# A mixture-of-experts kernel: low halves behind the weights' chunks, gates' transfers on another queue, transposes one turn sooner

## The chip, the cores and the metric

One core of one Trainium2 chip. The metric is the device time of one execution in microseconds (us). Of the engines TensorE (PE) multiplies, VectorE (DVE) and ScalarE (ACT) work element by element, GpSimd (POOL) does some small work and issues gathers, and SyncE (SP) issues most transfers. Each engine takes its instructions in the order in which the program lists them, and so does each engine's queue of transfers.

## The reference

Three stages follow each other. Only the second one is touched by the change.

```python
x = linear_attention(q, k, v, lam)            # (1536, 512), chunks of 128 tokens here
xn = x / (norm(x) + 1e-6); en = emb / (norm(emb) + 1e-6)
logits = xn @ en.T / tau                      # 8 experts
e = argmax(logits); gate = softmax(logits)[e]
for e in range(8):                            # experts: 512 -> 1024 -> 512
    out[mask] = gate * (relu(x[mask] @ w1[e]) @ w2[e])
h = out @ w_in                                # last MLP: 512 -> 2048 -> 512
y = elu(h) @ w_out
```

## The kernel before

Matrices that have to be exact to nearly float32 are held as two float16 parts, a high and a low half; one product is three matmuls (high by high, high by low, low by high). So each result that feeds another product is evicted twice: ACT writes the high half, and DVE, which reads that high half, writes the low half (`scalar_tensor_tensor`, L951 after the first layer, L988 after the second). The weights come as float32 in 1 MB pieces (`raw`) and are split in the same manner, in chunks of 128x1024: ACT writes the high half (L151), DVE the low half (L155). An expert has four pieces, two of `w1` (4e, 4e+1) and two of `w2` (4e+2, 4e+3); the last MLP's weights come as 64-bit numbers, and DVE first joins their bits in three instructions (L214, L217, L220).

`preparing` is a generator that lays these chunks one by one into the program; one step issues the high half of a chunk and the low half of the chunk before it. When a piece is finished its `end` issues the load of a later piece on SP's queue, which waits there until the buffer of the raw piece is free (five buffers, `rawp`). `tick(t)` gives a budget of `t` us and takes steps until it is spent: 1.6 after each of the four groups (`fp`) of the first layer, 3.7 after each of the two groups (`mp2`) of the second layer. `need(i)` takes further steps if a piece has not been laid out when matmuls use it.

The loop runs layer1(0), layer1(1), layer2(0), layer1(2), layer2(1), and so on, to layer1(7), layer2(6), layer2(7). In the profile L942 is the matmuls of the first layer (96 of an expert, 24 in a group) and L981 those of the second (96, 48 in a group). The tokens of an expert are gathered from DRAM by POOL (`gather`, L762, two tiles `g`) and are then transposed to `x`: for the experts 0 and 1 on PE, for the later ones by two transposing DMAs of SP (L921). `transpose(e+1)` and `gather(e+2)` are issued in layer1(e), after the second group (for e=0 after the third). A gather waits until the transposes of two experts before have read its buffer.

`route_sorted` (a second generator, `self.sorting`) works out each token's place and gate. One piece of it is taken after every other group of layer1 (the second and the fourth). One of them, taken after layer1(1), copies the counts and adds them up (L780 to L787), the one after layer1(5) writes the gates to DRAM (`cd`, L877) and reads them back to all partitions (`bc`, L880); both transfers are on SP's queue. The last MLP multiplies by `bc` first in L1033.

The sums of the experts go into `yT` (two tiles of 128 x 3520 four-byte words), which POOL sets to zero (L962) after the third group of layer1(0). `yT` is the first tile that is laid into the memory that the attention leaves; the attention's first pool there was `io`, four buffers of 8192 bytes per partition for the tiles `in`, against 28160 bytes of the two `yT`.

Of the kernel before, what the change touches and what calls it, by code (L numbers as in the profile page):

```python
# [9 lines left out]
F32 = mybir.dt.float32  # L10
# [10 lines left out]
P = 128  # L21
B, H, S, D = 2, 8, 768, 64
NP = H // 2
N, DM, E, FE, FF = 1536, 512, 8, 1024, 2048
# [40 lines left out]
class K:  # L65
# [702 lines left out]
    def route_sorted(self, a1, rhs, ps_r):  # L768
        nc, rt, cp = self.nc, self.rt, self.cp
# [39 lines left out]
        y = a1.tile([P, NS], F32, name="y")  # L809
# [64 lines left out]
        cs = a1.tile([44, P], F32, name="cs")  # L874
        nc.vector.tensor_copy(cs[32:44], sq[32:44])  # L875
        cd = self.dp.tile([12, P], F32, name="cd")
        nc.sync.dma_start(cd, cs[32:44])  # L877
        self.bc = cp.tile([P, N], F32, name="bc")
        ct = cd[:, :]
        nc.sync.dma_start(self.bc, bass.AP(tensor=ct.tensor, offset=ct.offset, ap=[[0, P], [1, N]]))  # L880
        yield
        self.overflow_table(a1)
        if "idx" in self.dbg:
# [6 lines left out]
    def moe_mlp(self, ctx):  # L890
        tc, nc = self.tc, self.nc
# [10 lines left out]
        def mm(shape, name):  # L902

            i = next(mms) % 4
            return self.ps_x.tile(shape, F32, name=name, tag=("xp", "kr")[i]) if i < 2 else ps_m.tile(shape, F32, name=name, tag="mm")

        W = N + CAP
        yT = []
        for hl in range(2):
            y = yp.tile([P, KD, W], F16, name=f"yT{hl}")  # L910
            yT.append(y)
        rhs = rp.tile([P, NS, 60], BF16, name="rhs")
        X, HT = self.X, {}

        def transpose(e):
            x = self.xp.tile([P, 2 * KD, CAP], F16, name=f"x{e}", tag="x")
            for j, n in ((0, P), (1, REM)):
                g = self.G.pop((e, j))
                o = x[:, :, j * P : j * P + n]
                if e > 1:  # L920
                    nc.sync.dma_start(o, g[:n].rearrange("p a d -> p (a d)"), transpose=True)  # L921
                    continue

                pt = ps_a.tile([P, 2 * KD, P], F16, name=f"pt{j}_{e}", tag="acc")
                for k in range(2 * KD):
                    nc.tensor.transpose(pt[:, k, :n], g[:n, k, :], self.id16[:n, :n])  # L926
                nc.scalar.activation(out=o, in_=pt[:, :, :n], func=AF.Copy)
            X[e] = x

        def layer1(e):  # L930
            x = X.pop(e)
            h = hp.tile([P, 2, E, CAP], F16, name=f"h{e}", tag="h")
            for fp in range(4):
                ps = mm([P, 2, CAP], f"ph{e}_{fp}")
                for j in range(2):
                    f = 2 * fp + j
                    w = self.need(4 * e + f // 4)
                    c = (f % 4) * P
                    n = 0
                    for k in range(KD):  # L940
                        for wl, xl in ((0, 0), (0, 1), (1, 0)):
                            nc.tensor.matmul(  # L942
                                ps[:, j, :], w[:, wl, k, c : c + P], x[:, xl * KD + k, :], start=(n == 0), stop=(n == 11)
                            )
                            n += 1
                    if e == 0 and f == 1:
                        self.route_end(ps_a)
                        self.tick(3.0)
                f2 = slice(2 * fp, 2 * fp + 2)
                nc.scalar.activation(out=h[:, 0, f2], in_=ps, func=AF.Relu)  # L950
                nc.vector.scalar_tensor_tensor(  # L951
                    out=h[:, 1, f2], in0=ps, scalar=0.0, in1=h[:, 0, f2], op0=ALU.max, op1=ALU.subtract
                )
                if fp % 2:
                    self.finished(4 * e + fp // 2)
                if e + 1 < E and fp == (1 if e else 2):
                    transpose(e + 1)
                    if e + 2 < E:
                        self.gather(e + 2)
                if e == 0 and fp == 2:  # L960
                    for y in yT:
                        nc.gpsimd.memset(y.bitcast(F32), 0.0)  # L962
                if e > 0 and fp % 2:
                    next(self.sorting, None)
                self.tick(1.6)
            HT[e] = h

        def layer2(e):
            h = HT.pop(e)
            offs = []  # L970
            for eng in (nc.scalar, nc.vector):
                offs.append(0 if e == 0 else eng.value_load(self.offi[0:1, e : e + 1], min_val=0, max_val=N))
            for mp2 in range(2):
                ps = ps_a.tile([P, 2, CAP], F32, name=f"py{e}_{mp2}", tag="acc")
                for j in range(2):
                    c = (2 * mp2 + j) * P
                    n = 0
                    for f in range(8):
                        w = self.need(4 * e + 2 + f // 4)
                        for wl, hl in ((0, 0), (0, 1), (1, 0)):  # L980
                            nc.tensor.matmul(  # L981
                                ps[:, j, :], w[:, wl, f % 4, c : c + P], h[:, hl, f, :], start=(n == 0), stop=(n == 23)
                            )
                            n += 1
                m2 = slice(2 * mp2, 2 * mp2 + 2)
                ya, yv = (yT[0][:, m2, bass.ds(o, CAP)] for o in offs)
                nc.scalar.activation(out=ya, in_=ps, func=AF.Copy, scale=EV_Y)  # L987
                nc.vector.scalar_tensor_tensor(  # L988
                    out=yT[1][:, m2, bass.ds(offs[1], CAP)], in0=ps, scalar=EV_Y, in1=yv, op0=ALU.mult, op1=ALU.subtract
                )  # L990
                if mp2 == 1:
                    self.finished(4 * e + 2, 4 * e + 3)
                self.tick(3.7)

        self.sorting = self.route_sorted(rp, rhs, ps_a)
        for e in range(E + 1):
            if e < E:
                layer1(e)
            if e > 0:
                layer2(e - 1)  # L1000
# [318 lines left out]
```

## Time and profile before

| | |
|---|---|
| median of 3 runs | 508.62 us (508.29 to 512.58) |
| profiled execution | 509.62 us, of which the span of the trace 507.8 us |
| PE busy in the span | 471.9 us (93%) |
| DVE, ACT, POOL busy | 347.1, 224.4, 77.1 us |
| mean granted TensorE clock | 0.979 |

The span is the time from the first to the last instruction of the trace. Times in rows are counted from the span's start. The attention lies before about 92 us, the experts from 92 to 250, the last MLP after that.

### The profile page before, as it was taken

How to read it: one execution, taken by the hardware profiler on the slowest of the kernel's cores; microseconds unless marked ns; L12 is line 12 of the kernel's file. 1: busy time of each engine (PE TensorE's matmuls, PEld its weight loads, DVE VectorE, ACT ScalarE, POOL GpSimd, SP SyncE). 2: the span in 40 equal slices, each digit the busy share in tenths (PEclk: the TensorE clock that was granted, in tenths of full speed). 3: DMA queues.
4: the chain of work that ended last, by engine and by line, in shares of the span. 5: the costliest groups of instructions: out<-in, count | busy, mean ns of one | idle time of the engine just before them, and what ended most of it. 6: DMA issues, size and time to landing. Idle time of an engine off the chain costs nothing.

```text
span 507.8 us, 9088 instructions
## 1 busy us (share of the span) xinstructions
PE 471.9 (93%) x3671; PEld 330.6 (65%) x3671; DVE 347.1 (68%) x625; ACT 224.4 (44%) x374; POOL 77.1 (15%) x67
## 2 busy tenths in 40 slices
PE   7788885998999999979999999999999999999992
PEld 6677775997999999979844444444444444445561
DVE  2467795466999988996878797978845335435352
ACT  1255344174686676423265354534333342433441
POOL 4456431351011310000000000000000002001111
PEclk9899898998999999999999999999999999999998
DMA  7999933267999999893622222000000001101101
GB/s 223 363 411 420 416 109 137 86 155 251 336 346 231 368 378 302 335 342 121 214 85 83 84 83 84 1 1 1 0 1 0 1 0 43 41 1 42 43 28 61
DMA packets 28335, 79.07 MB, mean 156 GB/s; under 512 B 13280, under 2 KB 15360, under 8 KB 22144
## 3 DMA queue, kind: packets, MB, share of 16 engines
q1 hardware_dynamic: 25848, 71.42, 41.4%
q0 software_dynamic: 2112, 6.82, 4.1%
q8 instruction: 31, 0.51, 0.4%
q10 hardware_dynamic: 328, 0.19, 0.1%
q14 instruction: 16, 0.13, 0.1%
HBM read 68.57 MB, written 7.10 MB: 149 GB/s over the span
## 4 chain that ended last, share of the span: by engine, by line
PE 77%; DVE 5%; DMA 3%; SPq 1%; issue 1%; ACT 1%; POOL 0%; POOLq 0%; DVEq 0%
PE pf L1023 25%; PE po L1063 24%; PE ph L942 14%; PE py L981 13%; DMA x<-g 2%; DVE w L155 1%; SPq L921 1%; DVE stm L352 1%; DMA g<-rows,idx 1%; PE px L712 1%; DMA out<-o,idx 1%; DVE S L422 0%; DVE row L452 0%; PE st L344 0%; PE pt L926 0%
## 5 line engine op out<-in xcount | busy, mean ns | idle before, releaser
L1023 PE MATMUL pf<-yT,w 128*128 128x512 f16 (+2 forms) x672 | 133.2, 349 | 0.0
L1063 PE MATMUL po<-w,g 128*128 128x512 f16 x576 | 133.1, 379 | 0.0
L1023 PEld LDWEIGHTS <-w 128*128 128x128 f16 x672 | 62.4, 98 | 65.4
L1063 PEld LDWEIGHTS <-g 128*128 128x128 f16 x576 | 55.9, 98 | 65.5 <-DVE g L1049 0.5
L1033 DVE TENSOR_TENSOR et<-pf,bc 128x512 f32<-128x512 f32 (+2 forms) x56 | 34.4, 614 | 91.5 <-PE pf L1023 91.4
L1034 ACT ACTIVATE eu<-et 128x512 f32<-128x512 f32 (+2 forms) x56 | 31.9, 569 | 140.0 <-DVE et L1033 140.0
L942 PE MATMUL ph<-x,w 128*128 128x224 f16 x768 | 75.2, 259 | 4.0 <-DMA x<-g 2.9
L981 PE MATMUL py<-h,w 128*128 128x224 f16 x768 | 76.6, 262 | 2.2 <-DVE w L155 2.2
L155 DVE SCALAR_TENSOR_TENSOR w<-raw,w 128x1024 f16<-128x1024 f32 x64 | 76.7, 1228 | 0.1
L981 PEld LDWEIGHTS <-w 128*128 128x128 f16 x768 | 74.2, 99 | 3.4 <-DVE w L155 2.4
L942 PEld LDWEIGHTS <-w 128*128 128x128 f16 x768 | 73.4, 98 | 4.7 <-DMA x<-g 3.1
L151 ACT ACTIVATE w<-raw 128x1024 f16<-128x1024 f32 x64 | 64.9, 1049 | 4.2 <-DVE cs L875 2.4
L1082 POOL DMA_INDIRECT out<-o,idx x12 | 11.8, 986 | 307.1 <-DVE o L1080 283.6
L762 POOL DMA_INDIRECT g<-rows,idx x16 | 22.1, 1383 | 84.3 <-DMA x<-g 58.8
L1049 DVE SCALAR_TENSOR_TENSOR g<-et,g 128x512 f16<-128x512 f32 (+2 forms) x56 | 34.1, 608 | 0.2 <-ACT g L1043 0.2
L1042 DVE SCALAR_TENSOR_TENSOR et<-eu,et 128x512 f32<-128x512 f32 (+2 forms) x56 | 33.9, 606 | 0.3 <-ACT eu L1035 0.3
L1035 ACT ACTIVATE eu<-eu 128x512 f32<-128x512 f32 (+2 forms) x56 | 31.9, 570 | 1.8
L1043 ACT ACTIVATE g<-et 128x512 f16<-128x512 f32 (+2 forms) x56 | 30.9, 553 | 0.3 <-DVE et L1042 0.3
L950 ACT ACTIVATE h<-ph 128x448 f16<-128x448 f32 x32 | 17.3, 541 | 21.4 <-PE ph L942 17.2
L951 DVE SCALAR_TENSOR_TENSOR h<-ph,h 128x448 f16<-128x448 f32 x32 | 19.8, 617 | 10.0 <-ACT h L950 9.9
L151 ACT ACTIVATE w<-cv 128x1024 f16<-128x1024 f32 x16 | 16.8, 1050 | 14.3 <-DVE cv L220 14.3
L987 ACT ACTIVATE yT<-py 128x448 f32 (+1 forms) x16 | 8.7, 545 | 32.2 <-PE py L981 32.2
(183 smaller groups left out, 403.4 us busy)
## 6 DMA issues: line engine op xcount, KB each, us to landing
raw<-w SPq DMA_DIRECT2D x32, 1024.0 KB, 7.9
in<-qkv SPq DMA_DIRECT2D x20, 512.0 KB, 7.6
raw<-wi SPq DMA_DIRECT2D x8, 1024.0 KB, 6.5
raw<-wo SPq DMA_DIRECT2D x8, 1024.0 KB, 7.9
rows<-row SPq DMA_DIRECT2D x15, 256.0 KB, 6.4
win<-qkv SPq DMA_DIRECT2D x4, 512.0 KB, 9.5
bc<-cd SPq DMA_DIRECT2D x1, 768.0 KB, 4.3
Dm<-Z SPq DMA_DIRECT2D x1, 512.0 KB, 3.9
```

The costliest lines, as they stand in the source:

```text
L151: nc.scalar.activation(out=o[0], in_=x, func=AF.Copy, scale=sc)
L155: nc.vector.scalar_tensor_tensor(out=o[1], in0=x, scalar=sc, in1=o[0], op0=ALU.mult, op1=ALU.subtract)
L942: nc.tensor.matmul(ps[:, j, :], w[:, wl, k, c : c + P], x[:, xl * KD + k, :], start=(n == 0), stop=(n == 11))
L981: nc.tensor.matmul(ps[:, j, :], w[:, wl, f % 4, c : c + P], h[:, hl, f, :], start=(n == 0), stop=(n == 23))
L1023: nc.tensor.matmul(ps[:, :n], w[:, wl, k, c : c + P], yT[yl][:, k, t0 : t0 + n], start=(i == 0), stop=(i == 11))
L1033: nc.vector.tensor_tensor(out=t[:, :n], in0=UT[m, f][:, :n], in1=self.bc[:, t0 : t0 + n], op=ALU.mult)
L1034: nc.scalar.activation(out=u[:, :n], in_=t[:, :n], func=AF.Relu, scale=-1.0)
L1035: nc.scalar.activation(out=u[:, :n], in_=u[:, :n], func=AF.Exp, scale=-1.0)
L1042: nc.vector.scalar_tensor_tensor(out=t, in0=u, scalar=-1.0, in1=t, op0=ALU.add, op1=ALU.max)
L1043: nc.scalar.activation(out=g[:, 0, :n], in_=t, func=AF.Copy, scale=S_G)
L1049: nc.vector.scalar_tensor_tensor(out=g[:, 1, :n], in0=t, scalar=S_G, in1=g[:, 0, :n], op0=ALU.mult, op1=ALU.subtract)
L1063: nc.tensor.matmul(acc[t], g[:, gl, t * P : t * P + P], w[:, wl, f % 4, :], start=(f == first and i == 0), stop=(f == last and i == 2),)
```

## The change

The low half after each group of either layer (L951, L988) is issued behind the `tick` of its group, and so behind the chunks that the tick lays out; in layer1 the pieces of `sorting` and the transposes and the next gather also come ahead of it. `transpose(e+1)` and `gather(e+2)` are issued after the first group instead of the second (for e=0 as before after the third). The two transfers of the gates go to GpSimd's queue. The zeros of `yT` are written as soon as `yT` exists, ahead of layer1(0).

```diff
@@ route_sorted
-        nc.sync.dma_start(cd, cs[32:44])
+        nc.gpsimd.dma_start(cd, cs[32:44])
         self.bc = cp.tile([P, N], F32, name="bc")
         ct = cd[:, :]
-        nc.sync.dma_start(self.bc, bass.AP(tensor=ct.tensor, offset=ct.offset, ap=[[0, P], [1, N]]))
+        nc.gpsimd.dma_start(self.bc, bass.AP(tensor=ct.tensor, offset=ct.offset, ap=[[0, P], [1, N]]))
@@ moe_mlp
             y = yp.tile([P, KD, W], F16, name=f"yT{hl}")
+            nc.gpsimd.memset(y.bitcast(F32), 0.0)
             yT.append(y)
@@ layer1
                 nc.scalar.activation(out=h[:, 0, f2], in_=ps, func=AF.Relu)
+                if fp % 2:
+                    self.finished(4 * e + fp // 2)
+                if e + 1 < E and fp == (0 if e else 2):
+                    transpose(e + 1)
+                    if e + 2 < E:
+                        self.gather(e + 2)
+                if e > 0 and fp % 2:
+                    next(self.sorting, None)
+
+                self.tick(1.6)
                 nc.vector.scalar_tensor_tensor(
                     out=h[:, 1, f2], in0=ps, scalar=0.0, in1=h[:, 0, f2], op0=ALU.max, op1=ALU.subtract
                 )
-                if fp % 2:
-                    self.finished(4 * e + fp // 2)
-                if e + 1 < E and fp == (1 if e else 2):
-                    transpose(e + 1)
-                    if e + 2 < E:
-                        self.gather(e + 2)
-                if e == 0 and fp == 2:
-                    for y in yT:
-                        nc.gpsimd.memset(y.bitcast(F32), 0.0)
-                if e > 0 and fp % 2:
-                    next(self.sorting, None)
-                self.tick(1.6)
@@ layer2
                 nc.scalar.activation(out=ya, in_=ps, func=AF.Copy, scale=EV_Y)
+                if mp2 == 1:
+                    self.finished(4 * e + 2, 4 * e + 3)
+                self.tick(3.7)
                 nc.vector.scalar_tensor_tensor(
                     out=yT[1][:, m2, bass.ds(offs[1], CAP)], in0=ps, scalar=EV_Y, in1=yv, op0=ALU.mult, op1=ALU.subtract
                 )
-                if mp2 == 1:
-                    self.finished(4 * e + 2, 4 * e + 3)
-                self.tick(3.7)
```

## Rows read from the trace of the kernel before

**Rows 1.** PE's waits: engine, line, whom it waited for: us in total, times, longest.

```profile
PE ph L942 <- DMA x<-g: 2.9, 1, 2.9
PE py L981 <- DVE w L155: 2.2, 1, 2.2
```

**Rows 2.** Timeline 106 to 123 us (start, us, engine, instruction, count; idle before and releaser).

```profile
111.23 1.05 ACT L151 ACTIVATE w<-raw 128x1024 f16<-128x1024 f32 x1
...
112.89 0.17 PE L777 MATMUL op<-ms,c 128*128 128x8 f16 x1
...
113.09 0.54 ACT L950 ACTIVATE h<-ph 128x448 f16<-128x448 f32 x1 [0.81 <-PE op L777]
113.67 0.62 DVE L951 SCALAR_TENSOR_TENSOR h<-ph,h 128x448 f16<-128x448 f32 x1 [0.55 <-ACT h L950]
114.21 0.15 DVE L780 COPY cnt<-op 128x8 f32<-128x8 f32 x1
...
115.92 2.35 DVE L155 SCALAR_TENSOR_TENSOR w<-raw,w 128x1024 f16<-128x1024 f32 x2
117.19 9.12 PE L981 MATMUL py<-h,w 128*128 128x224 f16 x76 [2.19 <-DVE w L155]
```

**Rows 3.** Stretches: us, busy of PE, PEld, DVE, ACT, POOL, PEclk, DMA share, GB/s.

```profile
115.00:117.10 2.10, 0.00 (x0) 0.00 (x0) 1.96 (x8) 0.53 (x1) 0.92 (x1) 1.00 0.73 128
...
117.80:121.20 3.40, 3.40 (x23) 2.75 (x21) 0.47 (x1) 0.00 (x0) 0.92 (x1) 0.55 0.98 393
...
222.00:225.00 3.00, 2.94 (x31) 2.97 (x32) 3.00 (x4) 1.09 (x2) 0.00 (x0) 1.00 0.95 393
```

**Rows 4.** Timeline 170 to 223 us: SP's queue, POOL, and the matmuls that wait.

```profile
170.05 5.87 SPq L921 DMA_TRANSPOSE x<-g  x2
...
180.07 1.60 POOL L762 DMA_INDIRECT g<-rows,idx  x1 [9.68 <-DMA x<-g]
...
194.99 0.64 SPq L877 DMA_DIRECT2D cd<-cs  x1
...
201.99 3.49 DVE L155 SCALAR_TENSOR_TENSOR w<-raw,w 128x1024 f16<-128x1024 f32 x3
203.94 0.35 SPq L880 DMA_DIRECT2D bc<-cd  x1
...
204.39 1.44 SPq L133 DMA_DIRECT2D raw<-wi  x2
...
205.92 1.61 SPq L133 DMA_DIRECT2D raw<-wo  x2
205.93 1.21 DVE L155 SCALAR_TENSOR_TENSOR w<-raw,w 128x1024 f16<-128x1024 f32 x1
...
207.63 9.00 SPq L921 DMA_TRANSPOSE x<-g  x2
...
222.06 9.36 PE L942 MATMUL ph<-x,w 128*128 128x224 f16 x96 [2.90 <-DMA x<-g]
```

**Rows 5.** Two stretches in the same columns as rows 3: SP waits for the gates, then not.

```profile
203.00:205.00 2.00, 2.00 (x23) 2.00 (x22) 2.00 (x3) 2.00 (x4) 0.00 (x0) 1.00 0.15 33
...
207.00:209.00 2.00, 2.00 (x23) 2.00 (x22) 1.79 (x9) 0.55 (x2) 0.00 (x0) 1.00 1.01 352
```

**Rows 6.** POOL's timeline, 82 to 183 us.

```profile
82.95 0.92 POOL L762 DMA_INDIRECT g<-rows,idx  x1 [0.30 <-issue]
95.73 0.97 POOL L762 DMA_INDIRECT g<-rows,idx  x1 [11.86 <-DVE idx L755]
...
100.40 6.03 POOL L962 MEMSET yT<- 128x3520 f32 x2
...
166.81 3.58 POOL L762 DMA_INDIRECT g<-rows,idx  x1 [0.30 <-issue]
```

**Rows 7.** Timeline 249 to 253 us: the end of the experts.

```profile
250.50 0.63 DVE L988 SCALAR_TENSOR_TENSOR yT<-py,yT 128x448 f32 x1 [0.86 <-ACT yT L987]
...
252.90 0.68 DVE L1033 TENSOR_TENSOR et<-pf,bc 128x512 f32<-128x512 f32 x1
```

## What the change is predicted to do

> **What bounds the kernel now.** Read PE first: it is busy for 93% of the span, so a change in the experts can only give back time in which PE stands still or runs at a low clock. The list of PE's own waits [rows 1] has two of size there: 2.9 us on a transposed `x`, and 2.2 us on the low half of a weights' chunk. The timeline places both. The weights' wait lies early in layer2(0), 115.00 to 117.19 [rows 2]; the other before layer1(7), 219.16 to 222.06 [rows 4]. After 250 us PE goes from matmul to matmul, and nothing in this change moves work there that PE waits for. A table of stretches, read last, shows what the clock made of the gaps: behind the first it was granted at 0.55 for 3.40 us (mostly its lower level, 1.2 GHz instead of 2.4), behind the longer second one it stayed at 1.00 [rows 3].
>
> **The low halves behind the chunks.** Nothing is added or removed; DVE's order changes. What is late at 117.19 is the first of the two L155 at 115.92 [rows 2]; it takes 2.35 / 2 = 1.18 us, ends at 117.10, and PE starts 0.09 later. Its input was there long before: ACT's half ended at 111.23 + 1.05 = 112.28. In front of it on DVE stand the low half of the last group (L951 at 113.67, which had waited for ACT) and the sums of the counts, 114.21 to 115.92 = 1.71 us. The sums need only the matmul L777, which ended at 112.89 + 0.17 = 113.06; ACT was released by it at 113.09, and I take 113.10 for DVE. With the low half behind, the chain is 113.10 + 1.71 + 1.18 + 0.09 = 116.08. The wait shrinks from 2.19 to 1.08: **gain 1.1 us**. Between 0 (DVE comes late from the groups before) and 2.19 I stay with 1.1, because the rows give every link. Late next are the sums of the counts, which stay in front.
>
> The clock comes on top. The 76 matmuls behind the gap take 9.12 us [rows 2]; 96 at the full clock take 9.36 us [rows 4], so 76 take 7.41. The low clock cost 1.7 us. With half the gap I expect it not to fall: **gain 1.7 us**, bounds 0 and 1.7, in the profiled execution. A 2.90 us gap left the clock alone, so the same gap may do so in another execution.
>
> The same order in every other group costs nothing. A low half of layer 1 now comes up to one or two chunks (1.2 us each) later; layer2(e) reads it after layer2(e-1) and layer1(e+1), two times 9.4 us further on, and the four buffers for these sums are taken again only in the next layer1. In layer 2 the second and third chunk of a tick also wait for ACT's halves, which queue behind ACT's eviction, so the low half can come some 4 us after its matmuls (0.54 + 2 x 1.05 + 1.2 + 0.1); only the last MLP reads it. The last one, after layer2(7), is where this cover ends. Today it runs from 250.50 to 251.13, with DVE idle for 0.86 us before it [rows 7], about when the eighth matmul of the MLP wants it. Now a chunk of 1.2 us and the first instruction of the next one stand ahead of it. Their inputs are there a group earlier, so I expect them in DVE's idle time and a cost of nothing; uncovered it is up to 1.9 us.
>
> **The gates' transfers.** On SP's queue `bc` waits until `cd` has landed: from the issue of `cd` at 194.99 to 203.94 nothing else is issued [rows 4]. The loads behind it go out in one burst, four of 1 MB from 204.39 to 207.53, and the transposes of expert 7 behind these at 207.63. The DMA engines show it: 33 GB/s in 203 to 205, then 352 in 207 to 209 [rows 5], so 4 MB are some 12 us of work in front of those transposes. They land at 222, 14.4 us after their issue began. For comparison, those of 170.05 were all read by POOL's gather at 180.07, 10.0 us [rows 4]. On POOL the two transfers stand behind the last gather and before nothing until the outputs. Their price there isn't in the trace; the nearest rows are POOL's gathers, 0.92 to 3.58 us each [rows 6], so 1.8 to 7.2 us of an idle engine. Even with some 12 us for the landing of each the gates are there before 225, and L1033 reads them at 252.90 [rows 7]: free.
>
> **The transposes a turn sooner.** For expert 7 they pass the tick of the first group, and with it one load, the fourth of the burst; its L155 ended at 205.93 + 1.21 = 207.14, and the transposes waited for that as well. They stay behind the third load, whose buffer the L155 run of 201.99 to 205.48 frees. So they go out at about 205.0 to 205.9 instead of 207.63, with less in front of them. 205.9 + 10.0 to 14.4 is 215.9 to 220.3, against 219.16 when PE wants them. I take the short end, as the queue will not have stood idle: **gain 2.9 us**; at the long end 1.8. Everything up to there hangs on PE's groups through ACT, so a PE that comes earlier brings the transposes earlier too; where they hold still, 216 stands against 216.4. For experts 2 to 6 nothing waits now, and a turn (2.3 us) more is cover. The load that falls behind the transposes goes out up to 9 us later. That is hidden by five raw buffers, and by weights that are ready well ahead after the first experts. The gathers go along a turn sooner and pass nothing on POOL.
>
> One rule speaks against the reason just given. The Trainium skill, "DMA: Bandwidth & Descriptors", section "Issuing engines are not separate DMA queues", says that transfers from any engine share the same DMA engines and that another issuer saves only sequencer time, usually small. Here the sequencer's time is 9 us of waiting on a landing, which the rule does not count; if only the issues of 0.64 and 0.35 us counted, the transposes' gain would be nearer rival B than my sum.
>
> **The zeros first.** The two memsets (6.03 us) move from 100.40 to behind the gather of 82.95, so to about 83.9 to 89.9, if the memory is free; it is that of the attention's `in` tiles, which none of its last steps reads. POOL then stands idle until 95.73 [rows 6]: free. The gather for expert 3 no longer waits for them, but PE doesn't want it.
>
> **Sum.** 1.1 + 1.7 + 2.9 = 5.7 us: 509.62 becomes 503.9 in the profiled execution (span 507.8 to 502.1). The median of the runs lies 1.0 below that execution. If that is the clock's doing there, only 1.1 + 2.9 = 4.0 is left, 504.6; if not, 5.7, 502.9. I forecast the middle, **503.7**.
>
> **Rivals.**
> A, forecast, 502.9 to 504.6: chance 0.58.
> B, the transposes are no earlier in effect: the DMA engines are busy anyway (share 1.01, [rows 5]), and the 2.9 us stay. 508.62 - 1.1 = 507.5 to 508.62 - 2.8 = 505.8, middle 506.6. Against it speaks the 33 GB/s stretch. Chance 0.14. The Trainium skill's sentence on issuing engines, above, would put the result here.
> C, the weights' wait stays whole, since the sums are the real chain or the chunk's DVE slot slips: 508.62 - 2.9 = 505.7. Against it: each link has its row. 0.08.
> D, more: the typical run also loses the clock at the longer gap, or the first wait goes whole: 508.62 - 5.7 - 1.1 = 501.8, and with 1.7 for the clock instead of the 1.1, 501.2. 0.14.
> E, slower: the memsets hold POOL. If their memory comes free only with the attention's end, they stand in front of the gather of expert 1 (95.73), whose transposes on PE come next in line. It decides when they start later than 95.73 - 6.03 = 89.7; the price is up to 6.0 us, and about 1.7 for the clock. With the transposes' 2.9 back and the weights' wait covered: 508.62 + 7.7 - 4.0 = 512.3. For it: both are in one queue, in this order. Against it: the `in` tiles were there, and they are done early. 0.06.
>
> **How the numbers follow.** A measurement of this kernel tells about 1% from no change: 503.5 and 513.7 are the bounds. Of A some 0.4 lies below 503.5 (0.23), D wholly (0.14): faster 0.37. E reaches 513.7 only with another mishap: of its 0.06 I give 0.04 to slower. The rest, 0.59, is within 1%. The range of 501.6 to 506.9 holds A, C, two thirds of B and half of D, 0.82.
>
> **What will show it.** Right: the L155 before the second group of matmuls of layer2(0) starts near 114.8, and PE's wait on `w` L155 is about 1.1; PEclk is 1.0 from 117 to 122; PE has no wait on `x<-g`; the transposes of expert 7 go out before the fourth load; the memsets stand at 84 to 90; the first L1033 comes at about 247 instead of 252.90. Wrong: a wait of PE on L988 at the MLP's start, on the gather of expert 1, or on `x` of another expert; or a low clock in a new place.

## The result and the profile after

| | before | after |
|---|---|---|
| median of 20 runs each | 509.17 us (505.70 to 514.35) | 504.47 us (500.06 to 509.91) |
| ratio, 95% interval | | 0.9899 (0.9876 to 0.9923) |
| profiled execution, its span | 509.62 us, 507.8 us | 506.57 us, 504.8 us |
| mean granted clock | 0.979 | 0.973 |
| experts: first matmul of layer1(0) to first of the last MLP | 157.3 us (92.37 to 249.66) | 150.9 us (91.93 to 242.86) |

The ratio makes it 5.1 us faster, between 3.9 and 6.3; the medians lie 4.7 apart. The ratios here leave out executions over 1.5% above the fastest of their kernel (4 of the 20 after); the medians count all. The forecast of 503.7 was a gain of 4.9.

PE's waits in the kernel after (engine, tile, line, whom it waited for: us in total, times, longest), those that lie in the experts:

```profile
PE py L980 <- DVE w L155: 1.1, 1, 1.1
...
PE ph L943 <- DVE x L742: 0.3, 1, 0.3
```

Against [rows 1]: the wait on the transposes is gone, and that on the chunk's low half is 1.1 us instead of 2.2. What lies between is in the timeline of the kernel after (start, us, engine, instruction, count; idle before and releaser):

```profile
82.82 6.03 POOL L911 MEMSET yT<- 128x3520 f32 x2
95.42 0.98 POOL L762 DMA_INDIRECT g<-rows,idx  x1 [6.57 <-DVE idx L755]
...
111.94 0.17 PE L777 MATMUL op<-ms,c 128*128 128x8 f16 x1
...
112.17 0.17 DVE L780 COPY cnt<-op 128x8 f32<-128x8 f32 x1 [1.13 <-PE op L777]
...
113.89 2.35 DVE L155 SCALAR_TENSOR_TENSOR w<-raw,w 128x1024 f16<-128x1024 f32 x2
115.17 7.46 PE L980 MATMUL py<-h,w 128*128 128x224 f16 x76 [1.13 <-DVE w L155]
116.17 0.62 DVE L962 SCALAR_TENSOR_TENSOR h<-ph,h 128x448 f16<-128x448 f32 x1
...
190.35 0.57 POOL L877 DMA_DIRECT2D cd<-cs  x1 [13.16 <-DVE cs L875]
192.82 3.94 SPq L133 DMA_DIRECT2D raw<-wi  x2
196.21 0.59 POOL L880 DMA_DIRECT2D bc<-cd  x1 [5.28 <-DMA cd<-cs]
199.89 0.33 SPq L133 DMA_DIRECT2D raw<-wo  x1
200.32 5.08 SPq L922 DMA_TRANSPOSE x<-g  x2
205.50 0.96 SPq L133 DMA_DIRECT2D raw<-wo  x1
...
215.26 9.36 PE L943 MATMUL ph<-x,w 128*128 128x224 f16 x96
...
243.64 0.63 DVE L990 SCALAR_TENSOR_TENSOR yT<-py,yT 128x448 f32 x1 [1.34 <-ACT yT L986]
245.65 0.69 DVE L1032 TENSOR_TENSOR et<-pf,bc 128x512 f32<-128x512 f32 x1 [1.38 <-PE pf L1022]
```

It is read from the top. The memsets (now L911) stand at 82.82 to 88.85, and the gather of expert 1 behind them waits for its indices, not for them. The sums of the counts (from L780) are now released by the matmul L777; L155 follows at once, and the low half of the last group (now L962) comes behind it at 116.17. Here the copy waits for PE, where in [rows 2] it stood behind a low half. The same 76 matmuls take 7.46 us instead of 9.12. On POOL, `bc` stands for 5.28 us until `cd` has landed; SP's loads meanwhile go out from 192.82 on. The transposes of expert 7 start at 200.32, 14.9 us before layer1(7) wants them, and ahead of the fourth load; before it was 11.5 us (207.63 to 219.16, [rows 4]). The second of them landed 6.1 us after its issue, some 6 us before 215.26. The first L1032 comes at 245.65, 7.25 sooner than in [rows 7].

The table of stretches (us, busy of PE, PEld, DVE, ACT, POOL, PEclk, DMA share, GB/s) answers to [rows 3] and [rows 5]:

```profile
82.00:86.00 4.00, 2.62 (x16) 2.03 (x16) 2.45 (x10) 1.58 (x4) 4.00 (x3) 0.50 0.35 115
...
115.20:122.50 7.30, 7.30 (x77) 7.30 (x78) 5.57 (x7) 3.38 (x4) 0.00 (x0) 1.00 0.80 288
203.00:205.00 2.00, 2.00 (x23) 2.00 (x21) 1.69 (x11) 0.80 (x2) 0.00 (x0) 1.00 1.07 431
```

The first row is taken up at the end. Behind the gap PEclk is 1.00, and in the stretch that moved 33 GB/s it is 431.

**Where the gain goes.** In the profiles the experts are 6.4 us shorter and the MLP starts 6.8 us sooner, but the span is only 3.0 shorter. The MLP is no longer than it was: PE's last group of matmuls starts at 489.15 instead of 495.96, again 6.8 sooner. The rest is lost behind PE, at the scatters of the output. The timeline of the kernel after, that last group and the last three scatters:

```profile
489.15 2.90 PE L1062 MATMUL po<-w,g 128*128 128x512 f16 x12
...
486.57 0.97 POOL L1081 DMA_INDIRECT out<-o,idx  x1 [2.52 <-DVE g L1048]
491.57 0.97 POOL L1081 DMA_INDIRECT out<-o,idx  x1 [4.03 <-DVE g L1048]
495.57 0.97 POOL L1081 DMA_INDIRECT out<-o,idx  x1 [3.03 <-DMA out<-o,idx]
```

The same in the timeline of the kernel before:

```profile
495.96 2.90 PE L1063 MATMUL po<-w,g 128*128 128x512 f16 x12
...
493.39 0.97 POOL L1082 DMA_INDIRECT out<-o,idx  x1 [2.52 <-DVE g L1049]
497.20 0.97 POOL L1082 DMA_INDIRECT out<-o,idx  x1 [2.85 <-DVE g L1049]
500.85 0.97 POOL L1082 DMA_INDIRECT out<-o,idx  x1 [2.68 <-DMA out<-o,idx]
```

After stood 4.03 us where before stood 2.85, and from its last scatter to the end of the span are 9.2 us, not 7.0. The row names DVE, but the start fits the landing of the scatter before it: the one of 486.57 landed at 490.80, 0.77 us before the next starts, and in the kernel before the landing was at 496.43, again 0.77 before 497.20. From PE's last matmul to the end of the span that makes 12.7 us after and 9.0 before. I call it the tail; whether it belongs to the kernel is among the questions below.

### The profile page after: what moved, and what is told of

It reads as the page before. It is cut to its first block, busy times and chain, and to the rows that moved or that the text cites. A ratio compares the mean times of both kernels' runs of the same rounds, so it can differ in the third digit from the quotient of the medians.

```text
span 504.8 us, 9102 instructions
## 1 busy us (share of the span) xinstructions
PE 472.4 (94%) x3671; PEld 331.9 (66%) x3671; DVE 347.1 (69%) x625; ACT 224.7 (45%) x374; POOL 75.8 (15%) x69
## 4 chain that ended last, share of the span: by engine, by line
PE 78%; DVE 5%; DMA 3%; issue 1%; POOL 0%; ACT 0%; POOLq 0%; DVEq 0%; ACTq 0%
PE pf L1022 25%; PE po L1062 24%; PE py L980 14%; PE ph L943 13%; DMA g<-rows,idx 1%; DVE w L155 1%; DMA rows<-row 1%; DMA out<-o,idx 1%; DVE row L452 1%; DVE S L422 0%; DVE stm L352 0%; PE st L344 0%; PE tm L429 0%; PE px L712 0%; DVE ohb L660 0%
## 5 line engine op out<-in xcount | busy, mean ns | idle before, releaser
L1032 DVE TENSOR_TENSOR et<-pf,bc 128x512 f32<-128x512 f32 (+2 forms) x56 | 34.4, 614 | 93.3 <-PE pf L1022 93.2
L155 DVE SCALAR_TENSOR_TENSOR w<-raw,w 128x1024 f16<-128x1024 f32 x64 | 77.4, 1229 | 7.5 <-ACT w L151 7.4
L980 PE MATMUL py<-h,w 128*128 128x224 f16 x768 | 74.9, 259 | 1.1 <-DVE w L155 1.1
L1081 POOL DMA_INDIRECT out<-o,idx x12 | 12.1, 1011 | 287.6 <-DVE o L1079 262.9
L762 POOL DMA_INDIRECT g<-rows,idx x16 | 19.4, 1211 | 81.4 <-DMA x<-g 61.8
L951 ACT ACTIVATE h<-ph 128x448 f16<-128x448 f32 x32 | 17.2, 541 | 18.0 <-PE ph L943 17.2
L962 DVE SCALAR_TENSOR_TENSOR h<-ph,h 128x448 f16<-128x448 f32 x32 | 19.8, 618 | 5.8 <-ACT h L951 5.3
```

The costliest lines, as they stand in the source:

```text
L155: nc.vector.scalar_tensor_tensor(out=o[1], in0=x, scalar=sc, in1=o[0], op0=ALU.mult, op1=ALU.subtract)
L980: nc.tensor.matmul(ps[:, j, :], w[:, wl, f % 4, c : c + P], h[:, hl, f, :], start=(n == 0), stop=(n == 23))
L1032: nc.vector.tensor_tensor(out=t[:, :n], in0=UT[m, f][:, :n], in1=self.bc[:, t0 : t0 + n], op=ALU.mult)
```

## The experiments

The theory: the change gives back three things, half of the chunk's wait (1.1), the low clock behind it (1.7) and the wait on the transposes (2.9). Its rivals: one part does it all, or the clock or the wait of the transposes is a matter of the execution. Four kernels do one part alone, four take one part back, two move something further, and both kernels were profiled once more. Each ratio is to runs of the kernel before on the same chip (medians 508.70 to 511.09).

| kernel | median, us | ratio (95%) | experts, us | wait on `w`, us | wait on expert 7's `x`, us | low clock behind | tail, us |
|---|---|---|---|---|---|---|---|
| before | 509.17 | | 157.3 | 2.2 | 2.9 | `w` | 9.0 |
| before, again | 514.59 (one run) | | 159.5 | 2.2 | 3.3 | both | 12.1 |
| low halves only | 505.93 | 0.990 (0.987 to 0.993) | 155.6 | 1.1 | 3.1 | `x` | 9.4 |
| gates only | 506.14 | 0.993 (0.990 to 0.995) | 153.5 | 2.2 | 0 | `w` | 9.6 |
| turn only | 505.34 | 0.992 (0.989 to 0.996) | 151.7 | 2.2 | 0 | none | 9.5 |
| zeros only | 508.56 | 0.997 (0.993 to 1.000) | 157.0 | 2.2 | 3.4 | `x` | 9.3 |
| all but gates | 504.42 | 0.991 (0.987 to 0.994) | 150.7 | 1.1 | 0 | none | 9.3 |
| all but turn | 503.76 | 0.989 (0.985 to 0.993) | 150.6 | 1.1 | 0 | none | 9.0 |
| all but low halves | 506.20 | 0.995 (0.991 to 0.998) | 153.3 | 2.2 | 0 | `w` | 11.8 |
| all but layer 2's low halves | 505.75 | 0.989 (0.986 to 0.993) | 151.5 | 1.2 | 0 | none | 9.6 |
| after | 504.47 | 0.990 (0.988 to 0.992) | 150.9 | 1.1 | 0 | none | 12.7 |
| after, again | 507.88 (one run) | | 151.5 | 1.1 | 0 | none | 12.3 |
| sorting behind the tick | 504.36 | 0.991 (0.988 to 0.995) | 149.4 | 0 | 0 | none | 9.7 |
| gates on ACT | 505.83 | 0.992 (0.988 to 0.995) | 151.5 | 1.1 | 0 | none | 8.9 |

The columns from the fourth on are from one profiled execution of each kernel, which need not be a typical one: with the low halves alone it was the slowest of nine (509.02 us), with the sorting behind the tick the fastest of seven (501.91). A low clock means that the matmuls behind that gap took 1.5 to 1.7 us longer than at the full clock.

**One part alone.** The low halves, in layer1 (the same move in layer2):

```diff
-                nc.vector.scalar_tensor_tensor(
-                    out=h[:, 1, f2], in0=ps, scalar=0.0, in1=h[:, 0, f2], op0=ALU.max, op1=ALU.subtract
-                )
...
                 self.tick(1.6)
+                nc.vector.scalar_tensor_tensor(
+                    out=h[:, 1, f2], in0=ps, scalar=0.0, in1=h[:, 0, f2], op0=ALU.max, op1=ALU.subtract
+                )
```

> Only the low halves stand behind the ticks; transposes, gates and zeros as before. My theory (the weights' wait at layer2(0) is DVE's order): PE's wait on w L155 falls from 2.2 to about 1.1 us and the clock stays at its upper level behind it (1.7 us in an execution in which it fell before). The gates' transfer is issued some 2 us sooner, since its copy no longer stands behind a low half, so the wait on the transposed x of expert 7 shrinks too, to between 0.5 and 2 us. In all 2 to 4.5 us faster. Rival (the gain is the SP queue's alone): the wait on w stays at 2 us or more and the time falls by less than 1 us.

Timeline of this kernel, the two waits and SP's queue before the second:

```profile
116.10 7.46 PE L981 MATMUL py<-h,w 128*128 128x224 f16 x76 [1.12 <-DVE w L155]
...
190.87 0.72 SPq L877 DMA_DIRECT2D cd<-cs  x1
199.98 0.35 SPq L880 DMA_DIRECT2D bc<-cd  x1
...
204.06 9.74 SPq L921 DMA_TRANSPOSE x<-g  x2
...
219.49 10.82 PE L942 MATMUL ph<-x,w 128*128 128x224 f16 x96 [3.14 <-DMA x<-g]
```

The chunk's wait is halved and the clock holds behind it, as the theory has it. I had expected the second wait to shrink to 0.5 to 2 us, and that failed: 3.14. From the issue of `cd` to that of `bc` SP took 9.1 us again (190.87 to 199.98), so the transposes went out 3.6 us sooner than in [rows 4] and were wanted 2.8 sooner; the second landed 15.3 us after the first one's issue. And this time the clock fell there: 10.82 us for 96 matmuls that take 9.36 at the full clock.

The gates' two transfers:

```diff
-        nc.sync.dma_start(cd, cs[32:44])
+        nc.gpsimd.dma_start(cd, cs[32:44])
...
-        nc.sync.dma_start(self.bc, bass.AP(tensor=ct.tensor, offset=ct.offset, ap=[[0, P], [1, N]]))
+        nc.gpsimd.dma_start(self.bc, bass.AP(tensor=ct.tensor, offset=ct.offset, ap=[[0, P], [1, N]]))
```

> Only the gates' two transfers go to GpSimd's queue. My theory (SP stood behind the gates' landing): the loads of the last MLP go out as their buffers come free, the transposes of expert 7 are issued at the same time as before or up to 0.5 us sooner (they still stand behind the fourth load) but land within 11 us instead of 14.4, and PE's wait on them falls from 2.9 to below 0.6 us; the wait on w stays at 2.2. 2.3 to 2.9 us faster. Rival, the rule that issuing engines share the same transfer engines: the transposes land no earlier than 1 us before, the wait stays at 1.9 us or more.

Timeline of this kernel:

```profile
116.12 9.12 PE L981 MATMUL py<-h,w 128*128 128x224 f16 x76 [2.20 <-DVE w L155]
...
206.51 5.72 SPq L921 DMA_TRANSPOSE x<-g  x2
...
217.87 7.35 PE L942 MATMUL ph<-x,w 128*128 128x224 f16 x75
```

The transposes go out only 1.1 us sooner than in [rows 4], at 206.51, but the loads ahead of them had gone out from 197.53 on instead of in one burst. Each lands 6.2 to 9.0 us after its own issue, the second at 216.22, and layer1(7) starts without a wait. It is close: some 1.6 us.

The turn:

```diff
-                if e + 1 < E and fp == (1 if e else 2):
+                if e + 1 < E and fp == (0 if e else 2):
```

> Only the transposes and gathers come a turn sooner. My theory: SP still stands until about 204 behind the gates, then three loads and the transposes of expert 7 at about 206.4 instead of 207.6 with 3 MB instead of 4 in front of them; PE's wait on them falls from 2.9 to between 0.5 and 1.7 us, the wait on w stays at 2.2. 1.2 to 2.4 us faster. Rival (the turn is what counts): the wait on the transposes is gone, 2.9 us faster.

Timeline of this kernel:

```profile
116.43 7.46 PE L981 MATMUL py<-h,w 128*128 128x224 f16 x76 [2.20 <-DVE w L155]
...
200.50 0.35 SPq L880 DMA_DIRECT2D bc<-cd  x1
...
202.53 9.71 SPq L921 DMA_TRANSPOSE x<-g  x2
212.34 0.52 SPq L133 DMA_DIRECT2D raw<-wo  x1
...
216.51 8.69 PE L942 MATMUL ph<-x,w 128*128 128x224 f16 x89
```

A miss on the other side: I had left a wait of 0.5 to 1.7 us, and there was none, as the rival had it. SP still stands until 200.50, and the first transpose still takes 12.4 us from issue to landing; but they pass one load and go out 14.0 us before layer1(7), not 11.5, and that is enough. So each of the two parts takes the whole wait alone, and their gains don't add. The line at 116.43 shows something else: 2.20 us of waiting, and the clock holds.

The zeros:

```diff
             y = yp.tile([P, KD, W], F16, name=f"yT{hl}")
+            nc.gpsimd.memset(y.bitcast(F32), 0.0)
...
-                if e == 0 and fp == 2:
-                    for y in yT:
-                        nc.gpsimd.memset(y.bitcast(F32), 0.0)
```

> Only the zeros of yT are written ahead of layer1(0). My theory: the two memsets stand at about 84 to 90, the gather of expert 1 starts at 95.7 as before, nothing else moves; no change within 0.3%. Rival (POOL's memset holds DVE's small operations or the gather of expert 1): PE reaches layer1(0) or the transposes of expert 1 up to 3 or 6 us later and the time rises by as much.

The memsets ran from 84.80 to 90.83, the gather of expert 1 came at 96.52 with its wait on the indices, and both of PE's waits stood as before. The ratio of 0.9965 just leaves out 1 (0.9997), and the profile shows nothing to which 1.8 us could be put down.

**One part taken back.** The whole change with the two `nc.gpsimd` back on `nc.sync`; with `fp == (1 if e else 2)`; with both low halves back in front of their `tick`:

> The whole change, but the gates' transfers stay on SP's queue. If the turn alone carries the transposes of expert 7 (as in the run with the turn only, where PE did not wait and they landed close to the need), PE's wait on them stays at or below 0.5 us, but they land 13 to 15 us after their issue instead of some 9 as in the whole change; the time is that of the whole change within 0.3%. If the gates are needed once PE comes 1.1 us sooner, the wait comes back with 1 to 3 us. The wait on w is 1.1 us.

> The whole change, but transposes and gathers after the second group as before. If the gates' move alone carries the transposes (as in the run with the gates only, landed 1.6 us before the need), PE's wait on x stays at or below 0.5 us and the time is that of the whole change within 0.3%. If the margin of 1.6 us doesn't hold with PE 1.1 us sooner, the wait is up to 1.5 us. The wait on w is 1.1 us.

> The whole change without the low halves behind the ticks. My theory: PE's wait on w is back at 2.2 us, with the low clock behind it in some executions and not in others; no wait on x. Its experts take 1.1 us longer than those of the whole change (150.9 us) where the clock holds, 2.8 where it falls: 152.0 or 153.7 us. Rival (the low halves do more than that one wait): another wait of PE appears, or the experts take 155 us and more.

One line from the timeline of each, in the same order: layer1(7) starts without a wait in the first two, layer2(0) after one in the third.

```profile
218.24 9.36 PE L943 MATMUL ph<-x,w 128*128 128x224 f16 x96
...
216.91 9.36 PE L943 MATMUL ph<-x,w 128*128 128x224 f16 x96
...
115.31 9.12 PE L979 MATMUL py<-h,w 128*128 128x224 f16 x76 [2.20 <-DVE w L155]
```

The first two are as fast as the whole change, by time and by profile: 150.7 and 150.6 us for the experts. What the second of the two parts adds is margin. With both, SP is through with the transposes' issue at 205.40, 9.9 us before they are wanted; without the gates' move at 213.22, 5.0 before 218.24 (when they land, its trace doesn't show). Without the turn they have landed at 213.44, 3.5 before 216.91; with both it was 6. Without the low halves the wait is 2.2 us again, the clock falls behind it and the experts take 153.3 us, 2.4 more than with the whole change: 1.1 of wait and 1.66 of clock, nearly. I had given 152.0 with a clock that holds and 153.7 with one that falls; it fell. In time it is 506.20, and the intervals of the two ratios overlap.

Only layer 2's low half taken back:

```diff
+                nc.vector.scalar_tensor_tensor(
+                    out=yT[1][:, m2, bass.ds(offs[1], CAP)], in0=ps, scalar=EV_Y, in1=yv, op0=ALU.mult, op1=ALU.subtract
+                )
                 if mp2 == 1:
                     self.finished(4 * e + 2, 4 * e + 3)
                 self.tick(3.7)
-                nc.vector.scalar_tensor_tensor(
-                    out=yT[1][:, m2, bass.ds(offs[1], CAP)], in0=ps, scalar=EV_Y, in1=yv, op0=ALU.mult, op1=ALU.subtract
-                )
```

> The whole change, but the low halves of the second layer stay in front of the tick (those of the first layer behind it). My theory: the one wait that the order shortens lies behind a group of the first layer, so PE's wait on w is 1.1 us, the clock behind it holds, and the experts take 150.8 us as in the whole change. Rival (both layers are needed): the wait on w is 1.5 us or more, or another wait of PE appears.

No difference from the whole change: the gain of the low halves is layer 1's alone. The 0.6 us by which its experts are longer are for the most part a wait of layer1(1) on ACT's copy of `x` (0.54 us, at 104.88); both profiles of the kernel before, the second one of after and that of the gates on ACT have that wait too.

**What is late next.** The prediction named the sums of the counts. Here they go behind the chunks as well:

```diff
+                self.tick(1.6)
                 if e > 0 and fp % 2:
                     next(self.sorting, None)
-
-                self.tick(1.6)
```

> The whole change, and the pieces of the sorting are issued behind the tick of their group as well (ahead of the low half). My theory: what is left of the wait on w (1.1 us) is the sums of the counts in front of the chunk; then the chunk that layer2(0) waits for ends near 112.6, before PE needs it near 114, PE's wait on w is gone, and the experts take 149.8 us instead of 150.9. Against the kernel before a ratio near 0.987. Rival (the chunk is late on its own, by ACT's half or the raw piece): the wait stays at 0.8 us or more. The gates are written some 2 us later, which nobody waits for.

Timeline of this kernel:

```profile
111.51 0.17 PE L777 MATMUL op<-ms,c 128*128 128x8 f16 x1
111.54 9.36 PE L979 MATMUL py<-h,w 128*128 128x224 f16 x96
...
113.23 1.23 DVE L155 SCALAR_TENSOR_TENSOR w<-raw,w 128x1024 f16<-128x1024 f32 x1 [1.07 <-ACT w L151]
114.38 0.16 DVE L780 COPY cnt<-op 128x8 f32<-128x8 f32 x1
```

The chunk at 113.23 no longer waits for the sums, and PE goes through all of layer2(0) in one run of 96. So the sums were the rest of the wait, as the prediction's chain had it. It has the shortest experts (149.4 us) and the shortest span (500.0 us, its fastest run); its ratio can't be told from that of the whole change.

**Which engine stands.** The gates' transfers on ACT instead of POOL:

```diff
-        nc.gpsimd.dma_start(cd, cs[32:44])
+        nc.scalar.dma_start(cd, cs[32:44])
...
-        nc.gpsimd.dma_start(self.bc, bass.AP(tensor=ct.tensor, offset=ct.offset, ap=[[0, P], [1, N]]))
+        nc.scalar.dma_start(self.bc, bass.AP(tensor=ct.tensor, offset=ct.offset, ap=[[0, P], [1, N]]))
```

> The whole change, but the gates' two transfers go to ScalarE's queue instead of GpSimd's. My theory (what costs is the engine that stands until the first transfer has landed, not the transfer): ScalarE stands for 5 to 9 us between the two issues near 190 to 200, its evictions and the weights' high halves come that much later, PE waits 0 to 4 us on a sum's buffer or later on a weight, and the experts take 151 to 155 us. Rival (another issuer only saves the issue): ScalarE goes on between the two issues and the experts take 150.8 us.

Timeline of this kernel:

```profile
190.37 0.32 ACTq L877 DMA_DIRECT2D cd<-cs  x1
196.79 0.35 ACTq L880 DMA_DIRECT2D bc<-cd  x1
197.19 1.06 ACT L151 ACTIVATE w<-raw 128x1024 f16<-128x1024 f32 x1 [8.97 <-DMA cd<-cs]
...
245.45 1.47 PE L1021 MATMUL pf<-yT,w 128*128 128x512 f16 x6 [1.94 <-DVE yT L989]
247.84 8.36 PE L1021 MATMUL pf<-yT,w 128*128 128x512 f16 x38 [0.92 <-DVE yT L989]
```

ACT computes nothing for 8.97 us. Of these it stands 6.1 us until `cd` has landed, from the end of that issue (190.69) to the issue of `bc`; the rest is the two issues and what came ahead of them. The chunks' halves behind it come that much later. SP is free, and expert 7's transposes are in time. But PE now waits twice on the last low halves (1.94 and 0.92), the place that the prediction called uncovered. So the same stand shows on three engines: 8.3 to 8.5 us on SP before a wait of 2.9 to 3.4, 6.1 on ACT with 2.9 at another place, 5.3 on POOL with none. That the late chunks of ACT bring the late low halves fits DVE's timeline there (chunks, pieces of chunks and low halves without a gap from 237.6 to 247.8), but wasn't tried by itself.

**The kernels once more.** Both unchanged, a second profile of each:

> The kernel before, profiled once more: waits of 2.2 us on w and of 2.5 to 3.5 us on the transposed x of expert 7; the experts take 153.9 to 157.5 us, depending on behind how many of the two waits the clock falls (1.7 us each, seen behind none, one or two of them).

> The changed kernel, profiled once more: a wait of 1.1 us on w, none on x, a full clock behind it, experts of 150.6 to 151.0 us. The output scatters at the end, of which two took 4.2 and 4.6 us to land in its first profile, land in 2.7 to 3.3 us, and the time from PE's last matmul to the end of the span is 9 to 9.6 us instead of 12.7.

Timeline of the kernel before, second execution:

```profile
116.97 9.12 PE L981 MATMUL py<-h,w 128*128 128x224 f16 x76 [2.25 <-DVE w L155]
...
222.19 11.02 PE L942 MATMUL ph<-x,w 128*128 128x224 f16 x96 [3.31 <-DMA x<-g]
```

The waits repeat to 0.4 us; the clock doesn't: this time it fell behind both gaps. After repeats its wait of 1.1 us and its clock. I had expected a tail of 9 to 9.6 us for after; it was 12.3, with waits of 4.69 and 3.91 us before the last two scatters, and the kernel before had 12.1. The long tail occurs in kernels with and without the change (12.1, 11.8, 12.7, 12.3 of fourteen profiles), and five kernels that hold nearly all of the change have 8.9 to 9.7. So no part of the change need bring it, though only 2 of the other 12 profiles have it. Why both profiles of after have it these runs don't tell.

## Why the prediction was right

**The chunk's wait** (1.1 of gain): right, link by link. The rest is 1.13 us, forecast was 1.08; the sums take 1.72 us from 112.17 to 113.89. They start 0.9 sooner than forecast, since layer1(0) itself began 0.44 sooner and layer1(1) lost its wait of 0.57 us on ACT's copy. Rival C is out. Of D, the first wait whole, nothing came in this kernel; it takes the sums behind the chunks as well.

**The clock** (1.7): 9.12 to 7.46 is 1.66 us in the two profiles. The doubt about it was in place and one number for it hides a chance. Counted over all profiles of this study, the clock fell behind the gap of 2.2 us in 4 of 6, behind the gap of 2.9 to 3.4 us in 3 of 4, and behind the gap of 1.1 us in none of 7. In these profiles the shortened gap gave back its length each time and the clock only sometimes.

**The transposes** (2.9): gone whole, with 6 us to spare. The second landed 9.0 us after the first one's issue, near the short end of 10.0 that the sum took. What the prediction didn't see is that the two edits each do it alone. Rival B, the DMA engines busy anyway, is out: the stretch of 33 GB/s was room, and the loads now fill it (431). By the rule of the Trainium skill that the prediction weighed ("DMA: Bandwidth & Descriptors", section "Issuing engines are not separate DMA queues"), the transfers share the DMA engines and another issuer saves little, only the time to issue. The sharing is not in question here, but more than that time was saved. The move of the gates saved SP 0.99 us of issuing (0.64 + 0.35, [rows 4]) and 8.3 us of standing between the two, and it is the standing that held the loads and the transposes back.

**The low halves elsewhere, the zeros, the gates on POOL** (nothing each): right. No wait on a low half at the MLP's start, none on the gather of expert 1 (rival E), none on `x` of another expert.

**The sum.** 5.7 us forecast for the profiled execution; the experts gave 6.4. Of these 1.1 + 1.66 + 2.9 = 5.66 are the three terms and 0.57 the wait on ACT's copy, which comes and goes. The span gave 3.0, because the tail took 3.8 back; no term of the sum spoke of the tail, and for the profiled execution the forecast span of 502.1 us missed by 2.7. By the ratio it is 5.1 us, between the 4.0 without the clock and the 5.7 with it. That the middle of the two came so close is in part luck: which of the unprofiled executions lost the clock, and how long their tails were, is not on record.

**What stays open.** Measured one by one, the low halves (1.0%), the gates and the turn (0.8% each, of which one counts) and the zeros (0.35%) come to more than the whole change (1.0%). The low halves alone are worth 3.6 to 6.6 us by their interval (expected were 2 to 4.5), while their profile gives back 1.7 us of the experts' length. That profile is of the slowest of their runs, 3.1 us above their median, with a low clock at the second gap, so it need not show what a typical run gains. An interval is some 0.6% wide, so part of it is spread, and the four parts share one set of runs of the kernel before, beside which the whole change was not run; the rest isn't explained. Nor is the first row of the table of stretches: in 82 to 86, ahead of layer1(0), the granted clock is 0.50 after, where the same stretch of before has 0.75. It isn't why the mean clock is lower after (0.973 to 0.979): the second profile of after has the same stretch and 0.979. Up to PE's last matmul it is 0.983 in both; the difference lies behind it, where the clock stood at 0.50 for the last 10.3 us of the span after (from 494.46) and for the last 4.0 before (from 503.84). The low clock ahead of layer1(0) lasted 10.2 us in seven of the eight profiles with layer 1's low half behind the chunks, and 6.8 in the eighth and in the six others, though a low half comes only in layer1 itself, behind that stretch. What it costs isn't shown: layer1(0) starts at 91.8 to 95.1 us behind the longer stretch and at 91.3 to 93.2 behind the shorter, and the experts' lengths leave that out.

## What to carry to other kernels

When two gaps of an engine are costed, ask of each edit whether it alone closes the gap; two edits on one wait buy one gain and some margin. A transfer that reads what another transfer wrote made the engine that issued it stand until the landing (here 4.7 to 8.5 us, on three engines), so it belongs on an engine with nothing behind it. And follow a gain to the end of the span: what PE gave back here was partly eaten, in the profile, by the scatters behind it.

## What the runs showed of the hardware

- **The length of a gap does not settle the granted clock behind it.** In one execution of the kernel before the clock fell behind 2.2 us of waiting (0.55, [rows 3]) and held behind 2.90 (9.36 us for 96 matmuls, [rows 4]); in its second execution it fell behind both (11.02 us for 96 behind 3.31). The turn alone has the same gap of 2.2 us, from 114.23 to 116.43, and this in its table of stretches:

```profile
117.80:121.20 3.40, 3.40 (x38) 3.40 (x36) 1.17 (x2) 1.82 (x3) 0.00 (x0) 1.00 1.00 384
```

- **An issue of a DMA transpose has no fixed length.** The two of expert 7 held SP's queue for 5.08 us after, for 9.74 with the low halves alone and for 9.00 in [rows 4]; from the first one's issue to the second one's landing it was 9.0 us after and 15.3 with the low halves alone.
- **Scatters of 0.97 us each end this kernel 8.9 to 12.7 us behind PE's last matmul.** Each starts only when the one before has landed (0.77 us behind the landing, in the rows of the tail above), and the idle time before the last three spreads from 2.5 to 4.7 us.
